# Grouped 1x1 convolution on one core: two buffers of transposed input instead of three, an output ring of 288 columns instead of 280, and the TensorE loop's leftover groups put in front of it

## The chip, the core and the metric

The kernel runs on one core of one Trainium2 chip. The metric is device time in microseconds (us). "PE" is TensorE's matmuls, "PEld" its weight loads, "DVE" VectorE, "ACT" ScalarE, "POOL" GpSimd, "SP" the engine that only issues loads. A "q" after an engine (ACTq) means its sequencer, which issues transfers and waits.

## The reference

```python
H = W = 512; G = 4; Cg = 48; C = 192; k = 1
x: (1, 512, 512, 192) bf16,  w: (1, 1, 4, 48, 48) bf16
out[b,h,w,g,d] = sum_c x[b,h,w,g,c] * w[0,0,g,c,d]
```

It is a matrix product of 262,144 pixels of 192 channels with four 48x48 blocks. It reads 100.7 MB and writes 100.7 MB and has few operations per byte.

## The kernel before

A "column" is one pixel on each of the 128 partitions, 384 bytes a partition. A "group" is four columns (512 pixels) and there are 514 groups; a "pair" is two groups and there are 257 pairs.

Loads go into an input ring of 240 columns, in pieces of 80. TensorE transposes a pair (24 matmuls a pair in all: 12 transposes, then 12 matmuls of the pair before), VectorE copies the transposed pair from PSUM to one of `NXS` buffers `xT_sb`, TensorE multiplies, ScalarE copies the result into the output ring, and stores leave from there.

```python
OGRID = (72, 140, 212, 280)      # where a store ends in the output ring
OCOLS = OGRID[-1]
LATE_PART = 40                   # size of the stores in the last 240 columns
LAST_PARTS = (24, 20, 16, 8)     # the last stores
NXS = 3                          # buffers of transposed input
```

Twice in the run, 48 columns are loaded and stored unevenly: these "partial" fields use only 120 of the 128 partitions, in blocks that are meant to give some DMA engines less work than others. A packet's record names no engine, but the trace before shows how narrow the blocks are: the rows of the two 16-partition blocks ran at most four at a time (102.1 to 116.0 us), and the first nine rows of the 12-partition block started in threes (at 107.8, 109.9 and 112.1 us).

```python
PARTIAL = (("sync", 0, 16, 4, 0), ("sync", 32, 16, 4, 0),       # queue, first row, rows, engines, columns less
           ("pool", 52, 44, 11, 0), ("pool", 20, 12, 3, 0), ("pool", 96, 32, 8, 0))
UNEVEN = (("sync", 0, 16, 4, 16), *PARTIAL[1:])
FRONT = ((6, ((48, PARTIAL), (32, FULL))), (11, ((48, UNEVEN), (32, FULL))))
```

TensorE's program is a loop of 30 pairs, run 8 times, with unrolled pairs before and after it:

```python
def loop_spans(units):
    ...
    first = max((run[0].g0 - 1) // 2, 1)                     # 9
    rounds = (run[-1].g1 - 2 * first - 2) // body            # 8
    out.append((first, body // 2, rounds))                   # 9 pairs, 30 pairs x8, then 8 more pairs
```

The order of work and the waits that matter:

```python
def transposes(pair):                    # L350
    for g in groups(pair):
        if g % 2 and pair:
            pe.wait_ge(e_done[(pair - 1) % NTOK], 1)     # VectorE's copy of the pair before is done
        ...
def step(pair):                          # TensorE
    transposes(pair + 1)
    matmuls(pair)                        # L370
# VectorE                                # L409
dve.wait_ge(t_done, pair + 1)
if pair >= NXS:
    dve.wait_ge(mm_done, 2 * (pair - NXS + 1))           # the buffer is free
dve.tensor_copy(xT_sb[pair % NXS]..., xT_ps...)
# ScalarE, for each group                # L446; stores are issued at L427
act.wait_ge(mm_done, g + 1)
...issue the stores that are complete; wait until the store that used this place has landed...
act.copy(out_columns(g)..., o_ps...)
```

## Time and profile before

| | before |
|---|---|
| median time | 477.64 us (477.41 to 480.43, 3 runs) |
| span of the profiled run | 476.1 us |
| PE / DVE / ACT busy | 91% / 52% / 82% |
| bytes moved | 201.57 MB, 423 GB/s over the span |
| time of the DMA packets, summed and divided by 16 engines | 472.6 us |

From the page of the kernel before: the share of time that the DMA engines were busy and the bytes moved, in 40 equal slices.

```profile
DMA  8999999999999999999999999999999999999996
GB/s 330 439 394 431 429 423 432 432 430 428 435 431 429 434 421 435 435 429 433 439 431 428 428 436 433 424 427 434 433 434 424 439 422 425 433 432 432 420 424 287
```

The same in stretches of the kernel before; the columns are the stretch in us, its length, busy us of each engine (with number of instructions), TensorE's granted clock, DMA share and GB/s.

```profile
36.00:440.00 404.00, 376.32 (x5411) 339.96 (x5409) 215.49 (x226) 339.12 (x452) 11.18 (x20) 0.97 1.01 431
440.00:464.00 24.00, 23.30 (x340) 20.71 (x338) 13.46 (x15) 21.06 (x29) 0.00 (x0) 1.00 0.99 419
464.00:472.00 8.00, 2.08 (x23) 1.28 (x20) 0.90 (x1) 3.46 (x5) 0.00 (x0) 0.81 0.95 396
```

The DMA engines are full from shortly after the start until about 472 us, at 431 GB/s. TensorE's high busy share (91%) does not show that it is the limit, and neither does the page's chain of work, which puts 48% of the span on TensorE. These are lines of the waits view before (who waited for whom, total us, times, longest us):

```profile
DVE xT_sb L409 <- PE xT_ps L350: 214.8, 257, 6.3
ACT oring L446 <- PE o_ps L370: 56.7, 135, 7.8
ACT oring L446 <- DMA out_dram<-oring: 15.2, 7, 3.4
```

ScalarE waits most for TensorE (56.7 us), but 15.2 us of its waiting is for stores to land, which is a wait for the DMA engines. And this is how ScalarE's timeline ends before (start us, duration us):

```profile
466.55 0.34 ACTq L427 DMA_DIRECT2D out_dram<-oring  x1
466.93 0.80 ACT L446 CAST oring<-o_ps 128x768 bf16<-128x768 f32 x1 [0.21 <-issue]
467.76 0.34 ACTq L427 DMA_DIRECT2D out_dram<-oring  x1
```

All compute is done at 467.8 us, when the last store is issued, but the last row of data moves until 475.2 us: about 7.4 us of stores stand in the queue at the end.

### The profile page before, as it was taken

What the parts mean: (1) busy time and instruction counts of PE and PEld (TensorE: products, weight loads), DVE (VectorE), ACT (ScalarE), POOL (GpSimd) and SP (SyncE); (2) the same over time, 40 slices, a digit from 0 to 9 for tenths busy, and PEclk for the clock granted to TensorE, in tenths of its full rate; (3) what the DMA queues carried; (4) which work ended last, traced back from release to release, by engine and by line L of the source; (5) the groups of instructions that cost most, each with busy time, mean ns of one, the idle gap of its engine ahead of it and who ended that gap; (6) DMA issues with size and microseconds to landing.
All of it is one profiled execution on the core that took longest, in us unless ns stands there. A gap on an engine that the chain in (4) does not pass through costs nothing.

```text
span 476.1 us, 13580 instructions
## 1 busy us (share of the span) xinstructions
PE 431.7 (91%) x6178; PEld 389.5 (82%) x6178; DVE 246.8 (52%) x258; ACT 388.3 (82%) x515; POOL 12.5 (3%) x28
## 2 busy tenths in 40 slices
PE   5999999999598999999998896999978979999991
PEld 5888888888597988888987796898877977988880
DVE  2655555555255555555554453555535545555550
ACT  2898899988477898999987785899968968988882
POOL 1000000200002000000000000200002000000000
PEclk9999999999889999999999997999989989999996
DMA  8999999999999999999999999999999999999996
GB/s 330 439 394 431 429 423 432 432 430 428 435 431 429 434 421 435 435 429 433 439 431 428 428 436 433 424 427 434 433 434 424 439 422 425 433 432 432 420 424 287
DMA packets 10674, 201.57 MB, mean 423 GB/s; under 512 B 2112, under 2 KB 2112, under 8 KB 2752
## 3 DMA queue, kind: packets, MB, share of 16 engines
q1 hardware_dynamic: 4320, 97.44, 48.0%
q10 hardware_dynamic: 5120, 97.42, 47.8%
q0 software_dynamic: 1216, 6.49, 3.3%
q8 instruction: 9, 0.15, 0.1%
q14 instruction: 9, 0.07, 0.0%
HBM read 100.68 MB, written 100.66 MB: 423 GB/s over the span
## 4 chain that ended last, share of the span: by engine, by line
PE 48%; DMA 39%; ACT 8%; ACTq 1%; issue 1%; another core or an unknown queue 1%; SPq 0%; POOLq 0%
DMA out_dram<-oring 29%; PE o_ps L370 28%; PE xT_ps L350 20%; DMA ring<-in_x_dram 9%; ACT oring L446 8%; ACTq L427 1%; SPq L320 0%; SPq L313 0%; ACTq L420 0%; POOLq L300 0%; POOLq L299 0%; ACTq L429 0%
## 5 line engine op out<-in xcount | busy, mean ns | idle before, releaser
L446 ACT CAST oring<-o_ps 128x768 bf16<-128x768 f32 x514 | 387.0, 801 | 78.6 <-PE o_ps L370 56.7
L409 DVE COPY xT_sb<-xT_ps 128x1536 bf16<-128x1536 bf16 x257 | 246.1, 958 | 214.8 <-PE xT_ps L350 214.8
L370 PE MATMUL o_ps<-wt,xT_sb 128*128 128x144 bf16 (+1 forms) x3084 | 289.5, 236 | 24.2 <-ACT oring L446 18.5
L370 PEld LDWEIGHTS o_ps<-wt,xT_sb 128*128 128x128 bf16 x3084 | 212.6, 99 | 63.2 <-ACT oring L446 54.3
L350 PE MATMUL xT_ps<-ident,ring 128*128 128x128 bf16 x3084 | 222.4, 222 | 7.9 <-POOLq L300 4.9
L350 PEld LDWEIGHTS xT_ps<-ident,ring 128*128 128x128 bf16 x3084 | 190.1, 100 | 10.9 <-POOLq L300 5.1
L286 POOL DMA_DIRECT2D fill<-in_x_dram x8 | 4.6, 573 | 350.5 <-PE xT_ps L350 233.1
L296 POOL DMA_DIRECT2D ring<-in_x_dram x6 | 3.3, 559 | 0.0
L307 POOL DMA_DIRECT2D out_dram<-oring x6 | 3.3, 556 | 0.0
L332 PE MATMUL o_ps<-w_sb,esel 48*128 48x48 bf16 x10 | 0.6, 210 | 2.7 <-DMA w_sb<-in_w_dram 2.7
L332 PEld LDWEIGHTS o_ps<-w_sb,esel 48*128 48x128 bf16 x10 | 0.5, 113 | 2.7 <-POOL esel L273 2.7
L402 DVE CAST wt<-o_ps 128x480 bf16<-128x480 f32 x1 | 0.7, 658 | 3.3 <-PE o_ps L332 3.3
L446 ACT ACT_TABLE_LOAD x1 | 1.3, 1283 | 0.8 <-PEq L466 0.8
L273 POOL TENSOR_SCALAR_AFFINE_SELECT esel<-esel 48x272 bf16<-48x272 bf16 x1 | 0.4, 402 | 0.0
L270 POOL MEMSET esel<- 48x272 bf16 x1 | 0.3, 317 | 0.3 <-POOLq L466 0.3
L277 POOL TENSOR_SCALAR_AFFINE_SELECT ident<-ident 128x128 bf16<-128x128 bf16 x1 | 0.3, 282 | 0.0
L271 POOL MEMSET ident<- 128x128 bf16 x1 | 0.2, 198 | 0.0
L466 POOL MEMSET const-float32-0.0<- 128x1 f32 x1 | 0.1, 98 | 0.3 <-issue 0.3
L466 POOL MEMSET const-bfloat16-1.0<- 128x1 bf16 x1 | 0.1, 101 | 0.0
L466 POOL MEMSET const-uint8-127<- 128x1 uint8 x1 | 0.1, 101 | 0.0
L466 POOL MEMSET const-float32-1.0<- 128x1 f32 x1 | 0.1, 98 | 0.0
## 6 DMA issues: line engine op xcount, KB each, us to landing
ring<-in_x_dram SPq DMA_DIRECT2D x22, 3840.0 KB, 26.0
out_dram<-oring ACTq DMA_DIRECT2D x11, 3456.0 KB, 39.5
out_dram<-oring ACTq DMA_DIRECT2D x10, 3264.0 KB, 39.6
out_dram<-oring ACTq DMA_DIRECT2D x3, 1920.0 KB, 21.1
out_dram<-oring ACTq DMA_DIRECT2D x1, 3840.0 KB, 44.7
ring<-in_x_dram SPq DMA_DIRECT2D x2, 1536.0 KB, 32.8
out_dram<-oring ACTq DMA_DIRECT2D x2, 1536.0 KB, 40.8
out_dram<-oring ACTq DMA_DIRECT2D x1, 2880.0 KB, 37.2
```

The costliest lines, as they stand in the source:

```text
L273: gp.affine_select(out=esel[:], in_=esel[:], pattern=[[-1, ECOLS]], compare_op=AluOpType.is_equal, fill=0.0, base=ESHIFT, channel_multipli ...
L286: gp.dma_start(dst, src).then_inc(fill_sem[k], 16)
L296: gp.dma_start(sbuf, dram).then_inc(ld_sem[ld_key[p.i, n]], 16)
L307: gp.dma_start(dram, sbuf).then_inc(st_sem[i][n], 16)
L332: last = pe.matmul(o_ps[:, NOB - 1, col:col + CG], lhsT=esel[:, s0:s0 + 128], rhs=w_sb[:, g, :], start=True, stop=True, skip_group_check=True)
L350: last = pe.transpose(xT_ps[:, g % NXP, j * 128:(j + 1) * 128], xg[:, j * 128:(j + 1) * 128], ident[:])
L370: last = pe.matmul(o_ps[:, v % NOB, c0_:c1_], lhsT=xs[:, j * 128:(j + 1) * 128], rhs=wt[:, WOFF[tc]:WOFF[tc] + (c1_ - c0_)], start=(tc == ...
L402: dve.tensor_copy(wt[:], o_ps[:, NOB - 1, 0:WCOLS]).then_inc(wc_sem, 1)
L409: dve.tensor_copy(xT_sb[pair % NXS][:, 0:n * 2 * UC].rearrange("p (g c) -> p g c", g=n), xT_ps[:, b0:b0 + n, 0:2 * UC]).then_inc(e_done[pa ...
L427: act.dma_start(dram, sbuf).then_inc(st_sem[i][n], 16)
L446: act.copy(out_columns(g).rearrange("p (u c) -> p u c", u=2), o_ps[:, v % NOB:v % NOB + 2, 0:UC]).then_inc(fa_done[g % (2 * NTOK)] if g < ...
L466: nc = _bacc.Bacc("TRN2", target_bir_lowering=False, num_devices=1)
```

## The change

The intent: one buffer of transposed input less frees 3,072 bytes a partition, which is exactly 8 columns of output ring; the regular stores become 72 columns each, where they alternated between 72 and 68 (36 stores in all, not 37); and the leftover pairs stand in front of the loop, so that after it only one pair is left.

```diff
-OGRID = (72, 140, 212, 280)
+OGRID = (72, 144, 216, 288)
-LATE_PART = 40
-LAST_PARTS = (24, 20, 16, 8)
+LATE_PART = 44
+LAST_PARTS = (12, 32, 16, 8)
-NXS = 3
+NXS = 2
@@ class Unit
-    def __init__(self, pieces):
+    def __init__(self, pieces, last):
...
-        self.regular = pieces[0].at % BIG == 0 and 4 * (self.g1 - self.g0) == BIG
+        self.regular = pieces[0].at % BIG == 0 and (last or 4 * (self.g1 - self.g0) == BIG)
@@ plan_units
-        units.append(Unit(rest[:n]))
+        units.append(Unit(rest[:n], n == len(rest)))
@@ loop_spans
-            rounds = (run[-1].g1 - 2 * first - 2) // body
+            rounds, rest = divmod(run[-1].g1 - 2 * first - 2, body)
...
-                out.append((first, body // 2, rounds))
+                out.append((first + rest // 2, body // 2, rounds))
```

## The prediction

> **What bounds the kernel now.** The 16 DMA engines. The stretch view gives a DMA share of 1.01 at 431 GB/s from 36 to 440 us; the packets' own times add up to 472.6 us per engine of a 476.1 us span. [...] TensorE and ScalarE (82%, 514 copies of 801 ns) have slack: their idle spells (ScalarE waits 15.2 us in all for stores to land, by the waits view) fall where DMA stays full. A load takes 26 us and a store 39.5 us from issue to landing, so both queues hold work. ScalarE issues the last store at 467.8 us with some 8 us of stores queued; the last DMA row ends at 475.2 us. Outside saturated DMA are 2.3 us at the start and some 3 us at the end, where the engines finish one by one (one works alone for the last 1.3 us).
>
> **What the change does.**
> - Two buffers of transposed input: the VectorE copy of pair p must wait for matmuls(p-2). TensorE's order is matmuls(p-2), transposes(p), matmuls(p-1), so they are done before the transposes that the copy waits for anyway. New wait: 0.
> - Ring 288: 8 columns, two groups (1.6 us), more run-ahead for ScalarE. Its 15.2 us of waiting shrinks to perhaps 8-14 us; store landing grows a little. Off the critical path, since DMA is full.
> - Stores of 72 instead of 72/68, 36 in all instead of 37. A 27648-byte row takes 1030 ns, a 26112-byte row 973: 26.8 bytes/ns both. 30720 bytes in 1138 ns against 15360 in 573 makes some 8 ns a row fixed (an estimate); one store less saves 8 rows an engine, under 0.1 us.
> - Leftover groups in front: the same number of unrolled pairs (9+30+8, now 16+30+1). The trace has nine 16 KB instruction fetches of 0.95 us, each on one DMA engine: seven before 72 us, two after the loop at 457.7 and 467.4 us. One moves to about 80 us; I expect the other to stay. [...] The DMA engine that fetches does the same work in total: gain 0 to 1.3 us, the lone stretch at the end.
> - Last stores (44,44,44,12,32,16,8) leave less queued around 463 us, but still about 5 us: no dry spell.
>
> **Prediction.** 477.2 us, range 475.6 to 478.8. Faster by over 2%: 0.01; within 2%: 0.98; slower by over 2%: 0.01. Bytes, rate of rows and number of fetches stay; only the end can give about a microsecond.
>
> **Right or wrong in the profile.** Right: DMA share 1.0 and about 431 GB/s in the middle; VectorE waits only for TensorE; ScalarE's wait for stores smaller with no matching drop of the time; one fetch fewer in the tail; the last DMA row within 1.5 us of before. Wrong: a fetch in every loop round, DMA share under 0.95 before 464 us, VectorE waiting for matmuls, or one DMA engine finishing several us late.
>
> **What would make it wrong.** The balance of the DMA engines: the partial groups' transfers are uneven by design, and 2 to 3 us more on one engine moves the end directly. Also a refetching loop, or a starved tail.

## The result, and the profile after

| | before | after |
|---|---|---|
| median of six runs, same rounds | 477.91 us | 477.28 us |
| lowest to highest | 477.14 to 480.43 | 476.89 to 477.90 |
| span of the profiled run | 476.1 us | 475.5 us |
| DMA packets' time / 16, rows of data only | 470.64 us | 470.60 us |
| last row of data ends | 475.2 us | 474.7 us |

The ratio is 0.9981, with a 95% interval of 0.9958 to 1.0005. A ratio is the mean time of one kernel's fast runs over that of the other's of the same rounds, so it is not quite the ratio of the medians. The interval holds 1: no difference is shown. (A second measurement, at the end of the experiments, gave 0.9997.)

The page after, DMA in 40 slices:

```profile
DMA  8999999999999999999999999999999999999997
GB/s 326 439 393 421 435 426 429 442 416 433 435 434 428 435 421 435 435 429 435 429 434 432 430 432 430 432 430 428 433 433 428 433 429 427 428 435 428 423 429 307
```

The stretches after:

```profile
36.00:440.00 404.00, 375.20 (x5463) 339.47 (x5462) 218.05 (x228) 342.81 (x455) 11.19 (x20) 0.99 1.00 431
440.00:464.00 24.00, 22.33 (x321) 19.51 (x318) 12.45 (x13) 21.37 (x30) 0.00 (x0) 1.00 0.99 425
464.00:472.00 8.00, 0.00 (x0) 0.00 (x0) 0.00 (x0) 0.76 (x1) 0.00 (x0) 0.69 0.92 387
```

The middle has the same 431 GB/s at the same full share. What did change is on the compute side: from 36 to 440 us TensorE now ran 5,463 matmuls, not 5,411, and after 464 us nothing is left for it. The waits after:

```profile
DVE xT_sb L409 <- PE xT_ps L350: 211.9, 257, 5.8
ACT oring L446 <- PE o_ps L370: 47.0, 116, 8.0
ACT oring L446 <- DMA out_dram<-oring: 17.7, 9, 3.9
```

VectorE still waits for the transposes (257 times, once a copy), and no wait of it for the matmuls has come in: two buffers cost nothing. ScalarE's wait for stores is not smaller. The end of ScalarE's timeline after:

```profile
463.58 0.34 ACTq L427 DMA_DIRECT2D out_dram<-oring  x1
463.96 0.80 ACT L446 CAST oring<-o_ps 128x768 bf16<-128x768 f32 x1 [0.28 <-issue]
464.79 0.34 ACTq L427 DMA_DIRECT2D out_dram<-oring  x1
```

The compute engines are done 3.0 us sooner (464.79 against 467.76), and the end of the data moved by 0.5 us. The rest of the 3 us became a longer queue of stores: 9.9 us of reserve, not 7.4.

The trace also lists the fetches of instructions (16 KB each, one DMA packet of 0.88 to 1.04 us). Their start times:

```
before: 17.3 26.2 35.3 44.0 52.4 61.1 71.3           457.7 467.4
after:  18.2 26.5 36.9 45.3 54.0 62.6 71.4 79.9 89.1
```

Nine in both, but none after the loop any more. (Nine smaller fetches of 8 KB, about 0.31 us each, stand in both traces too, on another queue.)

### The profile page after: what moved, and what is told of

It is laid out like the page before. It is cut to its first block, busy times and chain, and to the rows that moved or that the text cites. A ratio compares the mean times of both kernels' runs of the same rounds, so it can differ in the third digit from the quotient of the medians.

```text
span 475.5 us, 13580 instructions
## 1 busy us (share of the span) xinstructions
PE 427.4 (90%) x6178; PEld 386.3 (81%) x6178; DVE 246.8 (52%) x258; ACT 388.9 (82%) x515; POOL 12.5 (3%) x28
## 4 chain that ended last, share of the span: by engine, by line
PE 61%; DMA 19%; ACT 12%; another core or an unknown queue 3%; issue 2%; ACTq 1%; SPq 0%; POOLq 0%
PE o_ps L370 35%; PE xT_ps L350 26%; ACT oring L446 12%; DMA out_dram<-oring 10%; DMA ring<-in_x_dram 9%; ACTq L427 1%; SPq L320 0%; SPq L313 0%; ACTq L420 0%; POOLq L300 0%; POOLq L299 0%; ACTq L429 0%
```

## The experiments

The theory (A): the DMA engines are saturated, the compute side has slack, and the end is set by when the slowest of the 16 DMA engines has done its share. Rivals: (B) the loop's shift gives what gain there is; (C) the ring's size sets the time. Twelve kernels were run; each is compared with runs of the kernel before on the same chip. One more, the kernel after with three buffers, did not build: the memory ran out (384 bytes a partition needed, 64 left). So a buffer had to go for the ring to grow to 288.

### 1. Each half of the change alone

`loop_only` is the kernel before with only the edits of `Unit`, `plan_units` and `loop_spans`; `ring_only` has only the edits of the constants:

```diff
# ring_only, against before
-OGRID = (72, 140, 212, 280)
+OGRID = (72, 144, 216, 288)
-LATE_PART = 40
-LAST_PARTS = (24, 20, 16, 8)
-NXS = 3
+LATE_PART = 44
+LAST_PARTS = (12, 32, 16, 8)
+NXS = 2
```

> The kernel before with the leftover groups in front of the TensorE loop and nothing else. Theory A (DMA saturated; the TensorE side has slack, the end is set by how evenly the DMA engines finish): 477 to 478 us, ratio to before 0.997 to 1.001; no instruction fetch after the loop's exit, last DMA row within 1 us of 475.2 us. Rival B (the stall and fetches after the loop's exit made the small gain): ratio 0.998 or lower, the same as the whole change, and ScalarE's last store issued some 3 us sooner than 467.8 us.

> The whole change without the loop's shift: two buffers, ring of 288, stores of 72, the new last stores. Theory A: ratio to before 0.997 to 1.001, DMA share 1.0 from 36 to 440 us, two fetches after the loop. Rival B (loop made the gain): ratio 1.000. Rival C (the larger ring made it): ratio 0.998 or lower.

Measured: `loop_only` 0.9991 (0.9975 to 1.0008), median 477.73 us against 477.93; `ring_only` 0.9994 (0.9976 to 1.0011), median 477.57. Neither differs from before.

The traces say which half did what. The shift of the loop alone moves both late fetches (now at 79.7 and 89.2 us, none after), and the last store is issued at 468.2 us, no sooner than before: rival B expected 3 us sooner and falls. The ring alone leaves the fetches where they were (454.7 and 464.4 us) and brings the last store to 464.9 us: the lead comes from the ring and its stores. These are single profiles: in the second one of the kernel after (experiment 6) the lead is 1.6 us, not 3.0. Neither the lead nor the fetches were worth measurable time.

### 2. How much slack the double buffer has: one buffer

```diff
-NXS = 2
+NXS = 1
```

> The kernel after with one buffer of transposed input. The VectorE copy of pair p then waits for matmuls(p-1), which stand behind transposes(p) in TensorE's order. By the argument of the prediction two buffers cost nothing, but one puts the copy (0.96 us) between matmuls of successive pairs: about 0.9 + 0.96 + 0.2 = 2.06 us a pair, times 257 = 530 us (an estimate), so 515 to 550 us, DMA share well below 1. If the copies had enough slack even so (a rival), it stays at 477.

Measured: 650.4 us (ratio 1.361), a larger loss than expected. The timeline of this run has one pair every 2.46 us:

```profile
301.19 0.96 DVE L409 COPY xT_sb<-xT_ps 128x1536 bf16<-128x1536 bf16 x1 [1.50 <-PE o_ps L370]
302.20 0.51 PE L350 MATMUL xT_ps<-ident,ring 128*128 128x128 bf16 x6 [0.79 <-DVE xT_sb L409]
302.55 0.99 PE L370 MATMUL o_ps<-wt,xT_sb 128*128 128x144 bf16 x12
303.65 0.96 DVE L409 COPY xT_sb<-xT_ps 128x1536 bf16<-128x1536 bf16 x1 [1.50 <-PE o_ps L370]
```

My estimate had copy and matmuls in turn. The trace shows a third link: half of the next pair's transposes (six) wait for the same copy and stand in front of the matmuls. So the cycle is copy, six transposes, twelve matmuls, copy; 1.50 us of it is VectorE waiting for the matmuls. From two buffers on, this wait is not in the trace at all; with one it is in every pair but the first, as the waits view of this run has it:

```profile
DVE xT_sb L409 <- PE o_ps L370: 390.6, 256, 3.9
```

That confirms the prediction's argument about order, and that its danger would have been large.

### 3. Is it the bytes? Fewer bytes with the same instructions

```diff
                 for n, dram, sbuf in transfers(xf, ring, p, ("sync",)):
+                    if p.i >= 6 and p.full and p.size == BIG:
+                        sbuf, dram = sbuf[:, :72 * C], dram[:, :72 * C]     # load48: 48 * C
                     sp.dma_start(sbuf, dram)...
```

Both give wrong results (old input stays in part of the ring); every compute instruction stays.

> The kernel after, wrong on purpose: 19 of its 30 loads bring 72 of their 80 columns, 7.47 MB of 201.6 MB less; every instruction of the compute engines stays. Theory A: the time falls by those bytes at 431 GB/s, 17.3 us, to 458 to 462 us. A rival that has the compute engines or the ring's hand-overs as the limit: no drop, 475 us or more.

> Wrong on purpose: the same 19 loads bring 48 of 80 columns, 29.9 MB less. By bytes alone 69 us less, 408 us; but 514 copies of 801 ns on ScalarE with their gaps make about 421 us, with start and tail 430 to 450 us. So the compute limit should show at 430 to 450 us, DMA share below 1: that is the slack that the kernel has on the compute side (about 30 to 45 us).

Measured: `load72` 459.9 us, ratio 0.961; that is 17.4 us below the 477.28 us of the kernel after, for 17.3 expected from 7.47 MB at 431 GB/s. (The times are from different chips; each chip's runs of the kernel before had medians within 0.3 us.) `load48` 446.7 us, ratio 0.934, in the expected 430 to 450 us and far above the 408 us that bytes alone would give. In `load72` (first line) DMA is still full; in `load48` (second line) it no longer is:

```profile
200.00:420.00 220.00, 211.44 (x3098) 191.34 (x3096) 123.82 (x130) 194.72 (x259) 5.50 (x10) 0.99 1.01 430
200.00:420.00 220.00, 213.55 (x3159) 193.45 (x3157) 125.41 (x132) 198.47 (x264) 5.50 (x10) 1.00 0.94 381
```

In `load48` no wait of ScalarE for a store is left. So the kernel after is bound by bytes, and the compute side has some 30 us of slack (an estimate: 477 less 447). A change on the compute side cannot be seen within it, as long as stores are still queued when compute ends (experiment 4).

### 4. When does the ring's size matter?

```diff
-OGRID = (72, 144, 216, 288)
+OGRID = (72, 144, 216)          # ring216
+OGRID = (72, 144, 216, 252)     # ring252
```

> The kernel after with an output ring of 216 columns, three stores of 72, not four. Theory A: the ring only sets how far ScalarE runs ahead; stores are still always queued, so 477 to 479 us, ratio to before 0.997 to 1.003; landing of a store falls from 42.6 us to about 30. Rival C (ring size sets the time; 8 columns gave 0.6 us): 72 columns less give about 5 us more, ratio 1.01.

> The kernel after with an output ring of 252 columns (stores of 72, 72, 72 and 36). With 216 the last store was issued at 475.6 us and DMA ran dry before the end; with 288 at 464.8 us, 9.9 us before the last row. If the ring costs nothing as long as stores are queued at the end: last store issued at 469 to 472 us, DMA end within 1 us of 475 us, ratio to before 0.997 to 1.002. If the time follows the ring's size evenly (1.0093 at 216, 0.998 at 288): about 1.0037.

Measured: `ring216` 481.4 us, ratio 1.0093 (1.0055 to 1.0131), which is what rival C had said and outside what theory A allowed. `ring252` 477.9 us, ratio 0.9999 (0.9978 to 1.0020), where a time that follows the size evenly would be 1.0037. So the loss sets in somewhere between 216 and 252 columns and is not a slope over the whole range. (With 252 columns there are also 41 stores, not 36.) The stretches of `ring216` show where it is lost:

```profile
36.00:440.00 404.00, 369.12 (x5309) 334.32 (x5307) 211.61 (x222) 333.40 (x443) 11.18 (x20) 0.97 1.00 429
440.00:464.00 24.00, 23.20 (x340) 20.64 (x338) 13.62 (x15) 21.35 (x29) 0.00 (x0) 1.00 0.93 398
464.00:478.60 14.60, 9.33 (x133) 7.96 (x130) 4.79 (x5) 10.09 (x14) 0.00 (x0) 0.93 0.78 323
```

DMA is still full until 440 us, then it has gaps. The last lines of ScalarE's timeline, first for `ring216`:

```profile
475.59 0.34 ACTq L427 DMA_DIRECT2D out_dram<-oring  x1
```

and for `ring252`:

```profile
472.07 0.34 ACTq L427 DMA_DIRECT2D out_dram<-oring  x1
```

| ring (run) | last store issued, us | last row of data, us | reserve, us | ScalarE's wait for stores, us | ratio to before |
|---|---|---|---|---|---|
| 216 | 475.6 | 478.6 | 3.0 | 30.1 | 1.0093 |
| 252 | 472.1 | 475.7 | 3.6 | 24.7 | 0.9999 |
| 280 (before) | 467.8 | 475.2 | 7.4 | 15.2 | 1 |
| 280 (`loop_only`) | 468.2 | 475.8 | 7.6 | 19.3 | 0.9991 |
| 288 (`ring_only`) | 464.9 | 474.8 | 9.9 | 14.8 | 0.9994 |
| 288 (after) | 464.8 | 474.7 | 9.9 | 17.7 | 0.9981 |
| 288 (`after_again`) | 466.2 | 475.2 | 9.1 | 17.3 | 0.9997 |

The ring sets how far ScalarE may run ahead of the stores, and so when it is finished. The end of the run is the later of two things: the DMA engines' own end (about 475 us), and ScalarE's end plus the 3 us or so that the last small store takes (3.0 us in `ring216`, and 3.0 in `load48`, where DMA was not full either). At 216 the second is later; at 252 they nearly meet; from 280 on the first decides, and more ring only adds to the queue. ScalarE's last wait for a store ends at about the same time in `ring216` (first line) and in the kernel after (second line):

```profile
390.33 0.80 ACT L446 CAST oring<-o_ps 128x768 bf16<-128x768 f32 x1 [4.26 <-DMA out_dram<-oring]
392.79 0.80 ACT L446 CAST oring<-o_ps 128x768 bf16<-128x768 f32 x1 [3.37 <-DMA out_dram<-oring]
```

After it ScalarE runs without any such wait to the end. But by the count of its copies, `ring216` with 72 columns less of room has 414 groups done at that moment and the kernel after 428; 14 copies of 0.80 us are 11.2 us, and `ring216` ends 10.8 us later. Theory A holds with this condition added to it; "off the critical path" was true of this ring, not of every ring.

### 5. Is the end set by the slowest DMA engine?

`even` takes the uneven groups away: `FRONT = ()`, all transfers spread over all 128 partitions.

> The kernel after without the uneven transfers of the partial groups: every load and store spread evenly over all 128 partitions. If the end is set by the slowest DMA engine (Theory A), one engine that the uneven groups relieve now finishes far behind the others: 480 to 495 us, a lone engine in the last 5 us or more. If the uneven groups are only overhead (rival): 475 to 477 us.

Measured: 489.6 us, ratio 1.0242 (1.0218 to 1.0267). Its stretches:

```profile
440.00:464.00 24.00, 23.32 (x341) 20.77 (x339) 13.63 (x15) 20.98 (x29) 0.00 (x0) 1.00 0.95 403
464.00:478.00 14.00, 8.45 (x116) 7.07 (x114) 4.53 (x5) 9.39 (x13) 0.00 (x0) 0.90 0.63 257
478.00:488.00 10.00, 0.00 (x0) 0.00 (x0) 0.00 (x0) 0.00 (x0) 0.00 (x0) 0.50 0.06 23
```

A DMA share of 0.06, at 23 GB/s, is one sixteenth: from 478 us on, a single engine works and 15 have ended. The bytes are the same (the rows' packets take 470.6 us per engine, as in the kernel before), yet the run is 11.5 us longer (489.6 less 478.15 for the kernel before on that chip). So balance is worth more than anything in this change, and the uneven groups of the kernel before are what keeps it.

The trace also shows how the lag grows. Every transfer of this run ends with sixteen packets of 4 bytes (1,008 for its 63 transfers), as many as there are engines, so I take the distance between the last two of a load as the last engine's lag:

| last but one engine ends the load at, us | 105 | 175 | 244 | 330 |
|---|---|---|---|---|
| last engine's lag, us | 0.1 | 2.4 | 4.8 | 7.9 |

It grows by about 0.6 us a load, with no fetch of 16 KB in this stretch (the last of this run's eight is at 79.0 us), so these fetches are not its cause. Of the 1,643 store rows of 27,648 bytes between 110 and 330 us, 97 took 1.04 us or more (median 1.088), where most took 1.025: about one in sixteen, as if one engine's rows were slower. Of the 1,613 load rows of 30,720 bytes, 94 took 1.14 us or more (median 1.154), where most took 1.138. With eight rows an engine in each transfer that makes 0.50 and 0.13 us for a store and a load (an estimate from these medians), which is the growth seen. So it is most likely one engine that does its rows more slowly all along; why is not shown.

With that, could the balance be bettered? In the kernel after, the engine that ends last has the final 0.9 us to itself (from 473.7 to 474.7 us). `less24` takes 24 columns in both partial fields from the first block; `bal_a` and `bal_b` take 16 from the 12-partition block in the second, and leave the first block 4 or 36 columns less:

```diff
-UNEVEN = (("sync", 0, 16, 4, 16), *PARTIAL[1:])
+UNEVEN = (("sync", 0, 16, 4, 24), *PARTIAL[1:])                     # less24, in both fields
+UNEVEN = (("sync", 0, 16, 4, 4), ("sync", 32, 16, 4, 0),            # bal_a; bal_b: 36 for the 4
+          ("pool", 52, 44, 11, 0), ("pool", 20, 12, 3, 16), ("pool", 96, 32, 8, 0))
```

> The kernel after with another balance: 24 columns less in both partial fields for the first block of 16 partitions (four DMA engines), where it was 16 in one field. These engines get about 3.6 us less of work, the others about 0.2 us more each. Theory A: if the engine that ends last (474.7 us, others by 473.7) is among the four, the time falls by up to 1 us, ratio to before about 0.996; if it isn't, the time stays or rises by 0.2 to 0.5 us.

> The kernel after with another balance. Followed back from the end, the DMA engine that finishes last has rows of the partial groups' first and second transfers from GpSimd, so it is one of the three that the 12-partition block uses. That block gets 16 columns less in the second partial field (1.9 us less for those three), the first block of four engines 12 columns more (1.4 us). Balance theory: if that engine is rightly told, the last row ends up to 1 us sooner, ratio to before 0.996 to 0.998; if the four engines were already near the end, they now end last and nothing is gained (0.998 to 1.001).

> As the run of the same call with the 12-partition block lightened by 16 columns, but here the four engines of the first block get 20 columns less than in the kernel after (2.3 us less), and all engines 4 columns more of the last field (about 0.24 us). Balance theory with the late engine among the three: ratio to before 0.996 to 0.999. If it isn't: 0.999 to 1.002.

Measured: `less24` 1.0009 (0.9990 to 1.0028), `bal_a` 1.0001 (0.9981 to 1.0021), `bal_b` 0.9999 (0.9980 to 1.0019). None beats the kernel after or before. These trials were inconclusive. `less24` and `bal_b` changed more than the balance: they have one more group (515) and two more stores (38; three of 4, 8 and 4 columns near the end where the kernel after has one of 12), and issued their last store 4.5 and 2.9 us later than the kernel after. And the record of a DMA packet does not name its engine. I told the engines apart by chaining each packet to the one that ended just before it, and where two engines end a packet within a few ns of one another the chain can jump. Which engine is last in the kernel after stays open; `less24` gives a weak hint that it is none of the four of the first block (the last row ended at 475.9 us, not sooner), clouded by its extra group and stores.

### 6. The kernel after once more

> The kernel after once more, unchanged, to see whether its 0.6 us (ratio 0.9981, interval 0.9958 to 1.0005) is there again. If the change gives a small true gain: ratio 0.997 to 0.999. If it gives none: 0.999 to 1.001.

Measured: 477.66 us against 478.01, ratio 0.9997 (0.9971 to 1.0024). The last store was issued at 466.2 us and the last row ended at 475.2 us, as in the kernel before; all nine fetches stood before 90 us again. The 0.6 us of the first measurement is not confirmed.

## Why the prediction was right, point by point

- **Bound by the DMA engines: right, and shown.** The share stayed full at 431 GB/s in both kernels, and taking 7.47 MB away took the 17 us that they cost.
- **Two buffers cost no wait: right, and shown.** VectorE waits for the transposes alone after the change. One buffer would have cost 36%.
- **Time 477.2 us, within 2%: right** (477.28 and, measured again, 477.66). That the first median came within 0.1 us is luck, since single runs of the kernel after spread from 476.9 to 479.6 us; what the prediction foresaw is that nothing clear of the noise would change. The term "0 to 1.3 us" for the end came out as 0.5 us in the profiled pair of runs, but not clear of the noise: the two ratios are 0.9981 and 0.9997 with intervals that hold 1. In the second profile the last row ended no sooner than before (475.2 us).
- **The ring's 8 columns are two groups of run-ahead, 1.6 us:** the last store came 3.0 us sooner in the first profile (2.9 in `ring_only`) and 1.6 us sooner in the second. The new division of the last stores and run-to-run scatter are in that difference too.
- **"Its 15.2 us of waiting shrinks to perhaps 8-14 us": wrong.** It was 17.7 us (17.3 measured again, 14.8 in `ring_only`). The direction of the idea holds over a wide range: with 216 columns this wait is 30.1 us, with 252 it is 24.7, with 280 and 288 between 14.8 and 19.3. That is some 1.4 us for 8 columns (an estimate: 30.1 less 17.7, by nine), which is less than the scatter between two profiles of one ring size (15.2 and 19.3 at 280). So the fall was put too high, at up to 7 us, and what 8 columns do could not be seen. As long as stores stay queued to the end, such idle time costs nothing: a median of 477.28 us went with 17.7 us of it, one of 477.91 with 15.2.
- **One fetch moves and one stays in the tail: wrong.** Both left the tail, by the loop's shift alone. It cost nothing measurable: the number is nine in each, and `loop_only` ran at 0.9991.
- **"Off the critical path, since DMA is full": right for this change, but too general as a reason.** DMA being full now says nothing about a smaller ring; 216 columns cost 0.9%. What the profile should be asked is how much is queued when compute ends.
- **One buffer, 530 us (in the expectation of that run): too low,** because the transposes that wait for the same copy were left out of the cycle.
- **Balance named as the risk: right in kind.** Without it the run takes 11.5 us longer; this change did not touch it.

## What to carry to other kernels

When the DMA engines are full from start to end, ask of a change on the compute side only what it does to the reserve: the time from the last store's issue to the last row of data. Here a reserve of 7.4 us, well above one small store's landing time (3.0 us), meant that more buffer and earlier finishing were worth nothing, and that the next gain is in bytes (7.47 MB less took 17.4 us) or in how evenly the 16 engines end (11.5 us in `even`). Take idle time of an engine that is not the limit as a difference to the limit, not as time to be won.

## What stays open

- Equal work left one engine alone for the last 9 us of 487.5 in `even` (share 0.06 from 478 us on). That run had no transfer issued from GpSimd, and still one engine fell back by about 0.6 us a load from 105 to 330 us. Which engine it was, the trace does not say.
- Each fetch of 16 KB was one DMA packet of 0.88 to 1.04 us, nine in a run before and after (eight in `even`). What they cost the data is not shown here; they do not explain the late engine of `even`, whose lag grew from 0.1 to 7.9 us in a stretch without any of them.
- The kernel before runs its loop eight times over a body of some 1,440 matmuls and weight loads, and no fetch of 16 KB is recorded between 72 and 457 us. After the loop's shift, one fetch appears 3.0 us after the second round's first transpose (at 89.1 us) and none in the later rounds. When a fetch comes, and why that one does, no run shows.
